# Other places for the next batch's steps in batches 1 and 2 of an attention and feed-forward kernel

## The chip, the cores and the metric

The kernel runs on one core of a Trainium2 chip. The metric is the device time of one execution in microseconds (us); lower is better.

## The reference

Attention with projected keys and values, and behind it a feed-forward layer with a hard swish. Inputs are float32; q, k and v are [8 batches, 8 heads, 1024, 64], E and F are [64, 1024], w_in is [512, 2048], w_out is [2048, 512].

```python
k_proj = einsum('ks,bhsd->bhkd', E, k)
v_proj = einsum('ks,bhsd->bhkd', F, v)
scores = matmul(q, k_proj.transpose(0, 1, 3, 2)) / sqrt(64)
attn = exp(scores - max(scores)); attn = attn / (sum(attn) + 1e-09)
x = matmul(attn, v_proj).transpose(0, 2, 1, 3).reshape(8192, 512)
h = x @ w_in
out = (h * clip(h + 3.0, 0.0, 6.0) / 6.0) @ w_out
```

## The kernel before

The kernel works through the batches b = 0 to 7, each in two halves t = 0 and 1 of 512 tokens. While TensorE computes the feed-forward layer of batch b, the attention of batch b + 1 (`second`, a few steps for b + 2 as `third`) is put between its steps. Everything is issued in the order of the program; each engine takes its instructions in that order and waits by semaphores.

**The order.** A half is a written-out list of steps: `START` for the first half of batch 1, `ORDER` for the others of batches 1 and 2, `QUADS` from batch 3 on.

```python
    ORDER = ("L0 A7 L1 A6 L2 B7 L3 A1 L4 B2 L5 A3 L6 B5 L7 A4 "
             "L8 L9 B6 L10 N2 L11 B1 L12 N5 L13 B3 L14 L15 B4").split()
    START = "L0 B3 L1 L2 B4 L3 L4 L5 L6 L7 L8 L9 L10 N2 L11 L12 L13 N5 L14 L15".split()
```

- `Ln` is block n of 16 of the first layer (`first_group`): 8 matmuls of 128x64 weights by 512 tokens into a PSUM bank `mm` (four banks, the one that was freed first is taken next); then relu on ScalarE into `r` (L562), and on VectorE the product `g` (L563), which frees the bank. In batches up to 3, L0 and L1 of the first half are split: L0 takes the first three quarters of the contraction for two blocks (12 matmuls, two banks, xT of head pairs 0 to 2), L1 the last quarter of both (4 matmuls, head pair 3).
- `An`, `Bn` and `Nn` are the seven products (Strassen's) of the second layer for a pair of output blocks, 16 matmuls with 256 columns each. A and B belong to the half before, N to this one. Products 7, 2, 5 go to an `at` bank (four banks), which ScalarE copies (`m`, L692). Products 6, 1, 3, 4 add up in one `mm` bank, which VectorE reads between them: `o_sb<-m,mm` behind 6 and 1, `o_sb<-mm,m` behind 3; so 1 waits for the reading behind 6, 3 for that behind 1, 4 for that behind 3. A7 reads the half before's last eight blocks of `g`, block 15 last.
- `sums.c` (POOL, `sc<-g`, behind L7), `sums.a` (VectorE, `g<-g`: a long part behind N5 of START or B3 of ORDER, a short one at the start of the next half), `sums.b` (VectorE, `sb`) and `sums.d` (POOL, `sd`), both behind L0, make the operands of the products. `sc` is read first by N5, `sd` by A3.

**The attention of the next batch**, in the order in which it must run:

- `load_next`: POOL copies one element of the transposed queries (`mark`) and by that waits for their landing, then requests k, v (and q) of the batch after next. For batch 3, q is requested on its own (`behind_that`), behind a mark on the reciprocal sums.
- `projected`: 32 matmuls of keys and values into one `at` bank, two copies of the keys on ScalarE (`kp`), then entries in the list `later`, of which each L step issues one: `turn` (SyncE transposes `kp` into kT and q in two halves into qT, by DMA), the two copies of the values.
- `scores(j, ...)`: for each head pair j, 8 small matmuls into two `at` banks and two exponentials on ScalarE into `aT`; those of the first j at once, those of the second through `later`.
- `add_up(j)`: VectorE sums `aT` of j (`parts`, L308), after both of its exponentials.
- `spread(a, b)`: at a, VectorE turns the sums (L317 to L321); at b, it takes reciprocals (L326), and SyncE writes them to DRAM and reads them back spread over the partitions (`rec`), 8 transfers.
- `values(j)`: 4 matmuls into two `at` banks, and two multiplications by `rec` on VectorE into `xT` (L300) of the next batch.

`at((t, place), ...)` puts such steps behind a named step of half t; several at one place run in the order of their `at`.

Of the kernel before, what the change touches and what calls it, by code (L numbers as in the profile page):

```python
# [15 lines left out]
def kernel(  # L16
# [11 lines left out]
    nc = tc.nc  # L28
    B, H, S, D = q.shape
# [44 lines left out]
    def g_tile():  # L74
        return gpool.tile([P, FO, TOK], bf16, tag="g", name="g")
# [41 lines left out]
    def load_kqv(b, order="qkv"):  # L117
        kqv.setdefault(b, {})
        for n in order:
            kqv[b][n] = raw_tile(n)  # L120
            nc.gpsimd.dma_start(out=kqv[b][n], in_=kqv_dram[n][b])
# [10 lines left out]
    def add(out, x, y, engine=nc.vector):  # L132
        engine.tensor_tensor(out=out, in0=x, in1=y, op=ALU.add)  # L133

    def sub(out, x, y, engine=nc.vector):
        engine.tensor_tensor(out=out, in0=x, in1=y, op=ALU.subtract)  # L136
# [3 lines left out]
    v11, v12, v21, v22 = [w_in_sb[:, k:k + KX, f * P:(f + NQ) * P] for k in (0, KX) for f in (FO - 2 * NQ, FO - NQ)]  # L140
# [74 lines left out]
    def behind_that(last, *what):  # L215
        mark = att.tile([1, 1], bf16, tag="mark", name="mark")
        nc.gpsimd.tensor_copy(mark, last)
        load_kqv(*what)
# [3 lines left out]
    class Attention:  # L222
# [38 lines left out]
        def scores(self, j, *allocs):  # L261
            qT = qT_dma[self.b]
            tiles = [alloc() for alloc in allocs]
            for a in range(2):
                for t in range(NB):
                    for r in range(2):
                        nc.tensor.matmul(tiles[r][t * KP:(t + 1) * KP, a * HT:(a + 1) * HT],  # L267
                                         self.kT[r * D:(r + 1) * D, 2 * j + a, :],
                                         qT[r * D:(r + 1) * D, j, a, t * HT:(t + 1) * HT],
                                         start=True, stop=True)  # L270
            return tiles
# [23 lines left out]
        def values(self, j, *allocs):  # L295
            return self.quads(lambda r, h: self.vp[r:r + KP, h, :], j, allocs)
# [7 lines left out]
        def add_up(self, *js):  # L304
            if self.parts is None:
                self.parts = att.tile([P, KO, 32], f32, tag="parts", name="parts", bufs=1)
            for j in js:
                nc.vector.tensor_reduce(out=self.parts[:, j], op=ALU.add, axis=mybir.AxisListType.X, apply_transpose=True,  # L308
                                        in_=self.aT[j].rearrange("p a r n -> p (a r n)").rearrange(
                                            "p (c i) -> p c i", i=32))  # L310
# [239 lines left out]
    def behind_steps(n):  # L550
        return lambda f: soon.append([n, f])

    def step_done():
        for entry in soon:
            entry[0] -= 1
        for entry in [entry for entry in soon if entry[0] <= 0]:
            soon.remove(entry)
            entry[1]()
# [30 lines left out]
    def x_tile():  # L589
        return xpool.tile([P, KO, NB, TOK], bf16, tag="xT", name="xT")  # L590
# [42 lines left out]
    second = Attention(1)  # L633
    second.xT = x_next

    def pop():
        if later:
            later.pop(0)()
# [205 lines left out]
    second = Attention(2)  # L844
    for b in range(1, B):
        if b + 1 < B:
            x_next = second.xT = x_tile()
        third = Attention(b + 2) if b + 2 < B else None

        plan = {}  # L850

        def at(place, *what):
            plan.setdefault(place, []).extend(what)

        def scores(*js):
            return lambda: second.some_scores(js)

        def values(*js):
            return lambda: second.some_values(*js)

        def add_up(*js):
            return lambda: second.add_up(*js)

        def spread(turned, inverted):
            at(turned, lambda: second.sums_turned())
            at(inverted, lambda: second.spread_sums())

        if b == 1:
            at((0, "L2"), sums_of_w_in)
            at((0, "L0"), second.projected)  # L870
            at((0, "L8"), second.load_next)
            at((0, "N5"), scores(0, 1))
            at((0, "L15"), add_up(0))
            at((1, "L0"), add_up(1))
            at((1, "L1"), scores(2, 3))
            at((1, "L2"), add_up(2))
            at((1, "L3"), add_up(3))
            spread((1, "B2"), (1, "L5"))
        elif b == 2:
            at((0, "L2"), second.projected)  # L880
            at((0, "A4"), second.load_next)
            at((0, "A4"), scores(0, 1))
            at((0, "B6"), scores(2))
            at((0, "L10"), add_up(0))
            at((0, "B1"), scores(3), add_up(1))
            at((0, "B3"), add_up(2))
            at((1, "A6"), add_up(3))
            spread((1, "A1"), (1, "L4"))
            at((1, "L4"), third.projected)
        elif b + 1 < B:  # L890
            if b == 3:
                at((0, "L0"), lambda: add(v12, v12, v22, nc.gpsimd), lambda: sub(v21, v21, v22, nc.gpsimd))
                at((0, "start"), second.load_next)
            at((0, "L1"), scores(0, 1))
            at((0, "B7"), add_up(0))
            at((0, "A1"), scores(2, 3), add_up(1))
            at((0, "A3"), add_up(2))
            at((0, "A4"), add_up(3))
            spread((0, "B6"), (0, "B3"))
            if third:  # L900
                at((0, "B4"), lambda: third.projected(pause=False))
                if third.b + 1 < B:
                    at((1, "L7"), third.load_next)
        if b < 3:
            at((1, "N2"), values(0))
            at((1, "L12"), values(1))
            at((1, "B3"), values(2))
            at((1, "L14"), values(3))
            if b == 1:
                at((1, "B3"), lambda: behind_that(second.recs[1][:1, 0, :1], 3, "q"))  # L910
        elif b + 1 < B:
            at((1, "L3"), values(0, 1))
            at((1, "L7"), values(2, 3))

        def done(place):
            for f in plan.pop((t, place), ()):
                f()

        for t in range(NB):
            g = g_tile()  # L920
            sums = Sums(g)
            start = (b, t) == (1, 0)
            pairs = {"A": behind[0], "B": behind[1], "N": Pair(b, t, sums, 0, (b, t) == (B - 1, NB - 1))}
            quads = b > 2
            if quads:
                pairs["Q"] = Quad(xT, t, g, (b, t) == (B - 1, NB - 1))
            if not start:
                behind[0].sums.a(KH - left, KH)
            left = 2 * NQ if quads else 2
            done("start")  # L930
            for what in START if start else QUADS if quads else ORDER:
                n = int(what[1:])
                if what[0] != "L":
                    pairs[what[0]].step(n)
                    step_done()
                    if quads and what[0] in "LQB":
                        pop()
                    done(what)
                    if what == ("N5" if quads else "N5" if start else "B3"):
                        sums.a(0, KH - left)  # L940
                    continue
                if b < 4 and t == 0 and n < 2:
                    if n == 0:
                        first_two = TwoGroups(xT, t, g)
                    for fo in range(2):
                        first_two.part(fo, range(n * (KO - 1), KO - 1 + n))
                    if n == 1:
                        first_two.out()
                else:
                    first_group(xT, t, g, n, behind_steps(2) if quads and n >= KH else now)  # L950
                step_done()
                pop()
                if n == KH - 1:
                    sums.c()
                if not start and n == 0:
                    behind[0].sums.b()
                    behind[0].sums.d()
                if quads and n == 0:
                    pairs["Q"].sums()
                done(what)  # L960
            while soon:
                step_done()
            behind = [pairs["N"], Pair(b, t, sums, 1, (b, t) == (B - 1, NB - 1))]
        assert not plan, plan
        second, xT = third, x_next
# [37 lines left out]
```

## Time and profile before

| | us |
|---|---|
| median of 3 runs (480.66 to 480.93) | 480.84 |
| the profiled execution | 480.11 |
| its span, first to last instruction | 478.3 |
| PE busy in it | 471.1 |
| VectorE busy in it | 340.0 |
| POOL busy in it | 304.4 |
| ScalarE busy in it | 275.1 |

The granted TensorE clock is 1.000 over the span. PE is TensorE's matmuls, PEld its weight loads, DVE is VectorE, ACT ScalarE, POOL GpSimd, SP SyncE. A row of the timeline has the start and the length in us, the engine, the line of the kernel, the operation with what it writes and reads, and the number of instructions merged in it; in brackets stands the idle time of the engine before it and what ended it. The lengths of matmuls are modelled and overlap, so on PE the distance of the starts is the time that a step takes. A row of the form "DMA v<-in_v_dram" in the chain of waits has the start of the request and the time to the landing.

### The profile page before, as it was taken

Reading aid. Unit: us, or ns where it says so; the run is one execution under the profiler, and the core shown is the slowest. Engines: PE = TensorE matmul, PEld = TensorE weight load, DVE = VectorE, ACT = ScalarE, POOL = GpSimd, SP = SyncE. Lnnn points to the kernel's source line nnn. Section 1 sums busy time; section 2 is a strip of 40 time slices with the busy share of each in tenths; the row PEclk is TensorE's granted clock in tenths of the full one; section 3 lists DMA queues with packets and bytes.
Section 4 is the critical chain, followed back from the end, with each engine's and each line's share of the span. In section 5 each row is a group of like instructions: output and inputs, shape, how many; then the busy total and the mean of one; then the engine's idle time right before and its main releaser. Section 6 shows DMA issues by size and latency. Waiting matters only on the chain.

```text
span 478.3 us, 14964 instructions
## 1 busy us (share of the span) xinstructions
PE 471.1 (99%) x6450; PEld 347.1 (73%) x6450; DVE 340.0 (71%) x549; ACT 275.1 (58%) x532; POOL 304.4 (64%) x206
## 2 busy tenths in 40 slices
PE   8899999999999999999999999999999999999997
PEld 4454567667666776787787877778687877878797
DVE  3583387678765958886778867887778897747574
ACT  3666478775447554756466555666457554556451
POOL 8634956144335123877897778887778588788820
PEclk9999999999999999999999999999999999999999
DMA  9999989984976989995999197962931054111012
GB/s 165 197 201 207 239 148 209 161 152 95 226 148 109 208 158 223 201 202 135 222 143 194 48 210 144 209 135 67 210 117 45 24 151 120 45 47 45 30 62 89
DMA packets 84593, 68.65 MB, mean 144 GB/s; under 512 B 38320, under 2 KB 70576, under 8 KB 84528
## 3 DMA queue, kind: packets, MB, share of 16 engines
q0 software_dynamic: 33008, 29.36, 39.4%
q1 hardware_dynamic: 51152, 37.83, 33.0%
q8 instruction: 50, 0.82, 0.7%
q10 hardware_dynamic: 368, 0.52, 0.4%
q14 instruction: 15, 0.12, 0.1%
HBM read 71.83 MB, written 16.97 MB: 186 GB/s over the span
## 4 chain that ended last, share of the span: by engine, by line
PE 82%; DMA 7%; DVE 4%; POOL 2%; ACT 2%; issue 2%; SPq 1%; POOLq 0%; ACTq 0%
PE mm L199 60%; PE at L199 19%; DMA v<-in_v_dram 5%; DMA rec<-turned_rows 1%; PE at L288 1%; DVE g L563 1%; PE at L267 1%; DVE parts L308 1%; ACT aT L276 1%; SPq L335 1%; POOL q L103 1%; POOL k L107 1%; DMA turned_rows<-inv 0%; POOL v L107 0%; DVE xT L300 0%
## 5 line engine op out<-in xcount | busy, mean ns | idle before, releaser
L199 PE MATMUL mm<-xT,w_in_sb 128*64 128x512 bf16 (+1 forms) x1808 | 222.3, 375 | 0.0
L563 DVE SCALAR_TENSOR_TENSOR g<-r,mm 128x512 bf16<-128x512 f32 x216 | 146.1, 680 | 70.8 <-ACT r L562 69.8
L562 ACT ACTIVATE r<-mm 128x512 f32<-128x512 f32 x216 | 128.3, 598 | 114.6 <-PE mm L199 109.0
L199 PEld LDWEIGHTS <-w_in_sb 128*64 128x64 bf16 x2048 | 118.9, 110 | 58.3 <-issue 3.2
L199 PEld LDWEIGHTS <-g 128*64 128x64 bf16 x2048 | 113.5, 110 | 23.9 <-issue 4.1
L133 POOL TENSOR_TENSOR sc<-g 128x2048 bf16<-128x2048 bf16 x14 | 57.0, 4072 | 53.0 <-DVE g L563 53.0
L136 POOL TENSOR_TENSOR sd<-g,sb 128x1024 bf16<-128x1024 bf16 x28 | 59.0, 2126 | 42.4 <-DVE sb L136 40.0
L199 PE MATMUL mm<-w_out_sb,g 128*64 128x256 bf16 (+1 forms) x1088 | 78.1, 286 | 0.1
L199 PE MATMUL at<-w_sums,g 128*64 128x256 bf16 x896 | 59.0, 273 | 0.2 <-DVE g L563 0.2
L776 POOL TENSOR_SCALAR r<-r 128x512 f32<-128x512 f32 x27 | 41.5, 1536 | 15.2 <-ACT r L771 15.2
L692 ACT COPY m<-at 128x256 f32<-128x256 f32 x84 | 31.3, 373 | 32.8 <-PE at L199 28.1
L777 POOL TENSOR_TENSOR g<-r,qm 128x512 bf16<-128x512 f32 x27 | 36.3, 1345 | 2.3
L300 DVE TENSOR_TENSOR xT<-at,rec 128x512 bf16<-128x512 f32 x54 | 34.9, 682 | 2.6 <-DMA rec<-turned_rows 1.9
L199 PE MATMUL mm<-w_out_sb,sd 128*64 128x256 bf16 x480 | 31.4, 273 | 0.1
L136 DVE TENSOR_TENSOR o_sb<-m,mm 128x256 f32<-128x256 f32 x60 | 24.7, 412 | 9.5 <-PE mm L199 7.2
L199 PE MATMUL mm<-w_sums,sb 128*64 128x256 bf16 x480 | 31.3, 273 | 0.0
L276 ACT ACTIVATE aT<-at 128x512 bf16<-128x512 f32 x52 | 29.5, 602 | 2.9 <-PE at L267 2.9
L199 PEld LDWEIGHTS <-sd 128*64 128x64 bf16 x480 | 26.9, 110 | 4.0 <-issue 0.4
L308 DVE TRANSPOSE_TENSOR_REDUCE parts<-aT 128x32 f32<-128x1024 bf16 x24 | 29.6, 1234 | 0.0
L199 PE MATMUL at<-w_out_sb,sc 128*64 128x256 bf16 x448 | 29.6, 273 | 0.0
L199 PEld LDWEIGHTS <-sc 128*64 128x64 bf16 x480 | 26.7, 110 | 3.6 <-issue 0.5
L199 PEld LDWEIGHTS <-sb 128*64 128x64 bf16 x480 | 26.2, 110 | 4.2 <-issue 1.9
(115 smaller groups left out, 496.1 us busy)
## 6 DMA issues: line engine op xcount, KB each, us to landing
out_dram<-o_sb SPq DMA_DIRECT2D x60, 256.0 KB, 4.4
rec<-turned_rows SPq DMA_DIRECT2D x48, 256.0 KB, 5.8
k<-in_k_dram POOLq DMA_DIRECT2D x7, 1024.0 KB, 10.6
v<-in_v_dram POOLq DMA_DIRECT2D x7, 1024.0 KB, 16.3
q<-in_q_dram POOLq DMA_DIRECT2D x7, 1024.0 KB, 21.1
w_out_sb<-in_moe_w_out_dram POOLq DMA_DIRECT2D x4, 512.0 KB, 15.0
w_in_sb<-in_moe_w_in_dram POOLq DMA_DIRECT2D x7, 256.0 KB, 9.7
k<-in_k_dram POOLq DMA_DIRECT2D x4, 256.0 KB, 5.6
```

Source lines behind the costliest of these rows:

```text
L103: nc.gpsimd.dma_start(out=q0[:, t, hs], in_=kqv_dram["q"][0][:, hs, t * SB:(t + 1) * SB, :])
L133: engine.tensor_tensor(out=out, in0=x, in1=y, op=ALU.add)
L136: engine.tensor_tensor(out=out, in0=x, in1=y, op=ALU.subtract)
L199: nc.tensor.matmul(ps[lo:lo + width], stationary[:, lo:lo + width], moving, **flags)
L276: when(lambda r=r: nc.scalar.activation(aT[:, :, r, :], tiles[r].rearrange("p (a n) -> p a n", a=2), AF.Exp, scale=scale))
L300: when(lambda t=t: nc.vector.tensor_mul(self.xT[:, j, t, :], av[t], rec[:, t]))
L308: nc.vector.tensor_reduce(out=self.parts[:, j], op=ALU.add, axis=mybir.AxisListType.X, apply_transpose=True, in_=self.aT[j].rearrange("p a ...
L562: nc.scalar.activation(r, h_ps, AF.Relu, bias=0.5, scale=1.0 / 6.0)
L563: when(lambda: nc.vector.scalar_tensor_tensor(g[:, fo, :], r, 1.0, h_ps, op0=ALU.min, op1=ALU.mult))
L692: self.copy(m, ps)
L776: nc.gpsimd.tensor_scalar(out=r, in0=r, scalar1=1.0, scalar2=None, op0=ALU.min)
L777: nc.gpsimd.tensor_tensor(out=g, in0=r3, in1=h3, op=ALU.mult)
```

## The change

For the next batch's steps in batch 1 and in batch 2, the change gives other places in the lists. `ORDER`, `START` and all the steps themselves stay.

| step | batch 1 before | batch 1 after | batch 2 before | batch 2 after |
|---|---|---|---|---|
| projection of b + 1 | t0 L0 | t0 L6 | t0 L2 | t0 L0 |
| load_next | t0 L8 | t0 L12 | t0 A4 | t0 A1 |
| scores(0,1) | t0 N5 | t0 L14 | t0 A4 | t0 L9 |
| scores 2 and 3 | t1 L1 | t1 L1 | t0 B6; t0 B1 | t0 L14, as one |
| add_up(0), (1), (2), (3) | t0 L15, t1 L0, L2, L3 | t0 L14, t1 L0, L2, L3 | t0 L10, B1, B3, t1 A6 | t0 B6, N5, B4, t1 L1 |
| spread | t1 B2, L5 | t1 A1, B2 | t1 A1, L4 | t1 A1, B2 |
| values(0), (1), (2), (3) | t1 N2, L12, B3, L14 | t1 N2, B3, B3, B4 | t1 N2, L12, B3, L14 | t1 B1, N5, L13, B4 |
| q of batch 3 | t1 B3 | t1 B4 | | |
| projection of b + 2 | | | t1 L4 | t1 L6 |
| sums of w_in | t0 L2 | t0 B4 | | |

In batch 3, two operations of POOL on `w_in` go from t0 L0 to t0 A6. The condition `quads` is written in another way and is true in the same halves. The diff, with batch 3's lines and the conditions cut:

```diff
         if b == 1:
-            at((0, "L2"), sums_of_w_in)
-            at((0, "L0"), second.projected)
-            at((0, "L8"), second.load_next)
-            at((0, "N5"), scores(0, 1))
-            at((0, "L15"), add_up(0))
+            at((0, "B4"), sums_of_w_in)
             at((1, "L0"), add_up(1))
+            at((0, "L14"), scores(0, 1))
             at((1, "L1"), scores(2, 3))
+            at((1, "N2"), values(0))
+            at((0, "L12"), second.load_next)
+            at((0, "L14"), add_up(0))
             at((1, "L2"), add_up(2))
             at((1, "L3"), add_up(3))
-            spread((1, "B2"), (1, "L5"))
+            spread((1, "A1"), (1, "B2"))
+            at((1, "B4"), values(3))
+            at((0, "L6"), second.projected)
+            at((1, "B3"), values(1))
+            at((1, "B3"), values(2))
+            at((1, "B4"), lambda: behind_that(second.recs[1][:1, 0, :1], 3, "q"))
         elif b == 2:
-            at((0, "L2"), second.projected)
-            at((0, "A4"), second.load_next)
-            at((0, "A4"), scores(0, 1))
-            at((0, "B6"), scores(2))
-            at((0, "L10"), add_up(0))
-            at((0, "B1"), scores(3), add_up(1))
-            at((0, "B3"), add_up(2))
-            at((1, "A6"), add_up(3))
-            spread((1, "A1"), (1, "L4"))
-            at((1, "L4"), third.projected)
+            at((0, "B4"), add_up(2))
+            at((0, "B6"), add_up(0))
+            at((0, "L0"), second.projected)
+            at((0, "L9"), scores(0, 1))
+            at((1, "B4"), values(3))
+            at((1, "B1"), values(0))
+            at((0, "A1"), second.load_next)
+            spread((1, "A1"), (1, "B2"))
+            at((0, "L14"), scores(2, 3))
+            at((1, "L6"), third.projected)
+            at((0, "N5"), add_up(1))
+            at((1, "L1"), add_up(3))
+            at((1, "L13"), values(2))
+            at((1, "N5"), values(1))
...
-        if b < 3:
-            at((1, "N2"), values(0))
-            at((1, "L12"), values(1))
-            at((1, "B3"), values(2))
-            at((1, "L14"), values(3))
-            if b == 1:
-                at((1, "B3"), lambda: behind_that(second.recs[1][:1, 0, :1], 3, "q"))
```

More of the change, by code (lines that the diff above doesn't have):

```diff
@@ L868 @@
         if b == 1:
-            at((0, "L2"), sums_of_w_in)
-            at((0, "L0"), second.projected)
-            at((0, "L8"), second.load_next)
-            at((0, "N5"), scores(0, 1))
-            at((0, "L15"), add_up(0))
+            at((0, "B4"), sums_of_w_in)
             at((1, "L0"), add_up(1))
+            at((0, "L14"), scores(0, 1))
             at((1, "L1"), scores(2, 3))
+            at((1, "N2"), values(0))
+            at((0, "L12"), second.load_next)
+            at((0, "L14"), add_up(0))
             at((1, "L2"), add_up(2))
             at((1, "L3"), add_up(3))
-            spread((1, "B2"), (1, "L5"))
-        elif b == 2:
-            at((0, "L2"), second.projected)
-            at((0, "A4"), second.load_next)
-            at((0, "A4"), scores(0, 1))
-            at((0, "B6"), scores(2))
-            at((0, "L10"), add_up(0))
-            at((0, "B1"), scores(3), add_up(1))
-            at((0, "B3"), add_up(2))
-            at((1, "A6"), add_up(3))
-            spread((1, "A1"), (1, "L4"))
-            at((1, "L4"), third.projected)
+            spread((1, "A1"), (1, "B2"))
[4 more added lines that the diff above has]
+            at((1, "B4"), lambda: behind_that(second.recs[1][:1, 0, :1], 3, "q"))
+        elif b == 2:
+            at((0, "B4"), add_up(2))
[12 more added lines that the diff above has]
+            at((1, "N5"), values(1))
         elif b + 1 < B:
             if b == 3:
-                at((0, "L0"), lambda: add(v12, v12, v22, nc.gpsimd), lambda: sub(v21, v21, v22, nc.gpsimd))
                 at((0, "start"), second.load_next)
@@ L903 @@
                     at((1, "L7"), third.load_next)
-        if b < 3:
-            at((1, "N2"), values(0))
-            at((1, "L12"), values(1))
-            at((1, "B3"), values(2))
-            at((1, "L14"), values(3))
-            if b == 1:
-                at((1, "B3"), lambda: behind_that(second.recs[1][:1, 0, :1], 3, "q"))
-        elif b + 1 < B:
+        if 2 < b < B - 1:
             at((1, "L3"), values(0, 1))
             at((1, "L7"), values(2, 3))
+        if b == 3:
+            at((0, "A6"), lambda: add(v12, v12, v22, nc.gpsimd), lambda: sub(v21, v21, v22, nc.gpsimd))
         def done(place):
@@ L923 @@
             pairs = {"A": behind[0], "B": behind[1], "N": Pair(b, t, sums, 0, (b, t) == (B - 1, NB - 1))}
-            quads = b > 2
+            quads = (b, t) >= (3, 0)
             if quads:
```

## The prediction

> **What bounds the kernel now.** I read the page first.
>
> ```profile
> span 478.3 us, 14964 instructions
> PE 471.1 (99%) x6450; PEld 347.1 (73%) x6450; DVE 340.0 (71%) x549; ACT 275.1 (58%) x532; POOL 304.4 (64%) x206
> ```
>
> PE is busy 99% of the span, and the change removes no matmul and adds none. So it can win only what PE loses between its steps in batches 1 and 2, and lose only by new waits there. The next view is therefore the timeline of PE over those batches, read by the starts of rows (ends overlap). Columns: start, length, engine, line, operation, operands, count.
>
> ```profile
> 98.48 1.04 PE L199 MATMUL at<-w_out_sb,sc 128*64 128x256 bf16 x16
> 99.45 0.94 PE L267 MATMUL at<-qT,kT 64*64 64x256 bf16 x16
> 100.32 2.78 PE L199 MATMUL mm<-xT,w_in_sb 128*64 128x512 bf16 x24
> 102.93 1.13 PE L199 MATMUL at<-w_sums,g 128*64 128x256 bf16 x16
> 103.90 1.03 PE L199 MATMUL mm<-xT,w_in_sb 128*64 128x512 bf16 x8
> 104.86 0.63 PE L267 MATMUL at<-qT,kT 64*64 64x256 bf16 x16
> 105.42 1.06 PE L199 MATMUL mm<-w_out_sb,g 128*64 128x256 bf16 x16
> ...
> 111.62 1.06 PE L199 MATMUL mm<-xT,w_in_sb 128*64 128x512 bf16 x8
> 112.79 1.06 PE L199 MATMUL mm<-w_out_sb,sd 128*64 128x256 bf16 x16
> ...
> 115.40 1.06 PE L199 MATMUL mm<-xT,w_in_sb 128*64 128x512 bf16 x8
> 116.58 1.06 PE L199 MATMUL mm<-w_out_sb,g 128*64 128x256 bf16 x16
> ```
>
> These are, in order, N5, scores(0,1), L14 with L15 and the next L0 (24 matmuls), A7, L1, scores(2,3), A6, then L5, A3, L7, A4 of batch 1. Three L steps take 102.93 - 100.32 = 2.61 us, so a step is 0.87 us; a product step streams as many columns and takes the same. Whatever exceeds 0.87 is loss. After L5, A3 should start at 112.49 and starts at 112.79: 0.30 lost. A4 should start at 116.27 and starts at 116.58: 0.31 lost. A7 takes 0.97: 0.10 lost. A visit of two score groups costs 105.42 - 103.90 - 0.87 = 0.65 undisturbed, but 100.32 - 98.48 - 0.87 = 0.97 behind N5: 0.32 lost. A loss of this kind is all the change can move.
>
> **Visits put together.** The same timeline, later: B3 to L14 with one values visit between; B6 to L10 with one score group; an L step and the product after it, with two values groups between (batch 3).
>
> ```profile
> 127.07 1.04 PE L199 MATMUL mm<-w_out_sb,sd 128*64 128x256 bf16 x16
> ...
> 128.38 1.05 PE L199 MATMUL mm<-xT,w_in_sb 128*64 128x512 bf16 x8
> ...
> 149.88 1.04 PE L199 MATMUL mm<-w_out_sb,g 128*64 128x256 bf16 x16
> ...
> 151.19 1.05 PE L199 MATMUL mm<-xT,w_in_sb 128*64 128x512 bf16 x8
> ...
> 225.46 1.03 PE L199 MATMUL mm<-xT,w_in_sb 128*64 128x512 bf16 x8
> ...
> 226.97 1.06 PE L199 MATMUL mm<-w_sums,sb 128*64 128x256 bf16 x16
> ```
>
> A single visit costs 1.31 - 0.87 = 0.44 of either kind, two together 1.51 - 0.87 = 0.64: every visit pays about 0.2 for turning to the smaller tiles and back. Batch 2's scores(2,3) as one visit save 2 x 0.44 - 0.65 = 0.23. Batch 1's values(1) and values(2), now both at B3, save 0.24. **-0.47.**
>
> **Batch 1, first half.** scores(0,1) goes from behind N5 to behind L14. Its 0.32 was a wait for N5's bank, which ScalarE copies while L14 now runs: gone. What is late next is L15's product on VectorE, because add_up(0) is now queued ahead of it (it was queued behind it) and waits for both exponentials.
>
> ```profile
> 99.90 1.08 ACT L276 ACTIVATE aT<-at 128x512 bf16<-128x512 f32 x2
> 101.42 0.60 ACT L562 ACTIVATE r<-mm 128x512 f32<-128x512 f32 x1 [0.43 <-PE mm L199]
> ...
> 103.02 0.69 DVE L563 SCALAR_TENSOR_TENSOR g<-r,mm 128x512 bf16<-128x512 f32 x1 [0.29 <-ACT r L562]
> 103.63 1.24 DVE L308 TRANSPOSE_TENSOR_REDUCE parts<-aT 128x32 f32<-128x1024 bf16 x1
> ```
>
> The first two rows are of the timeline of ScalarE, the others of VectorE. Relu follows an L step by 0.23 (L14 ended at 101.19). New order: N5 ends 99.35, L14 100.22, visit 100.87, L15 101.74, L0 102.61; A7 reads L15's block in its last eighth, 103.37. Relu of L14 100.45; exponentials start about 0.49 later and 0.49 apart, the second ends 102.0; add_up(0) 102.05 to 103.25; L15's product ends 103.9. A7 loses 0.6 where 0.32 + 0.10 was lost: **+0.2**. The wait has no cover on PE. Its ends are 0 (the sum fits into VectorE's idle time) and 1.24 (all of it stands ahead); the worked value lies between.
>
> scores(0,1) also needs kT and the first half of qT, and the projection moves from L0 to L6.
>
> ```profile
> 85.30 1.06 ACT L241 CAST kp<-at 64x512 bf16<-64x512 f32 x2 [3.06 <-PE at L199]
> 139.21 1.23 SPq L250 DMA_TRANSPOSE kT<-kp  x1
> DMA to landing us min/median/max: 4.5/6.0/9.2
> ```
>
> The rows: ScalarE's copies of the keys, SyncE's issue of kT, and the answer for the tile qT. From the projection's end to scores(0,1) are ten steps, 8.7 us; the chain is 0.24 + 1.06 + 1.23 + 6.0 and some 0.1 of handover, 8.6. I take no further wait from the median (k and v of batch 3 are requested only when it has landed); at 9.2 it would be 3 us, at 4.5 none. The Trainium skill's page "DMA: Bandwidth & Descriptors", section "Latency and other measured facts", gives DMA transposes 261 GB/s; by it a half (512 KB) would land in an estimated 2.0 us and this wait be impossible. The trace's shortest is 4.5, so the trace decides and the wait stays a rival.
>
> **Batch 1, second half.** A3 and A4 wait for VectorE to read the bank that they add to: both start as the subtraction before them ends.
>
> ```profile
> 112.36 0.38 DVE L136 TENSOR_TENSOR o_sb<-m,mm 128x256 f32<-128x256 f32 x1
> ...
> 116.17 0.35 DVE L136 TENSOR_TENSOR o_sb<-mm,m 128x256 f32<-128x256 f32 x1
> ```
>
> VectorE is behind there because four sums of 1.24 lie in its queue. The change starts the first at 102.05 instead of 103.63. Chaining the same operations at the pitch of before, L15's product ends at 103.9 as it did (103.71), but one sum is then already done: everything behind is about 1.0 us earlier, while PE is 0.2 later. Then A1's subtraction ends at 112.1 (needed 112.6), A3's at 115.95 (needed 116.1). The turned sums move to A1 and the reciprocal to B2, ahead of L4's and L5's products; their banks are wanted a microsecond later still. Both waits go, the second narrowly: **-0.6** (ends 0 and -0.7). The spread's transfers start about 1.2 earlier; values(0), which is not moved, only gains.
>
> **From batch 1 to 2.** PE from L0 of batch 2, then VectorE before it.
>
> ```profile
> 131.47 1.47 PE L199 MATMUL mm<-xT,w_in_sb 128*64 128x512 bf16 x12
> 132.76 0.94 PE L199 MATMUL at<-w_sums,g 128*64 128x256 bf16 x14
> 133.88 0.30 PE L199 MATMUL at<-w_sums,g 128*64 128x256 bf16 x2 [0.19 <-DVE g L563]
> 134.02 0.60 PE L199 MATMUL mm<-xT,w_in_sb 128*64 128x512 bf16 x4
> ...
> 128.35 0.68 DVE L563 SCALAR_TENSOR_TENSOR g<-r,mm 128x512 bf16<-128x512 f32 x1
> ...
> 129.29 1.29 DVE L300 TENSOR_TENSOR xT<-at,rec 128x512 bf16<-128x512 f32 x2
> 130.49 0.95 DVE L136 TENSOR_TENSOR g<-g 128x1536 bf16<-128x1536 bf16 x1
> 131.36 0.68 DVE L563 SCALAR_TENSOR_TENSOR g<-r,mm 128x512 bf16<-128x512 f32 x1
> ```
>
> A7 takes 1.26: 0.39 lost, since values(3)'s multiplications stood ahead of L15's product. They now stand behind it, and the projection of batch 3 (L0 instead of L2) lies between L0 and A7: gone. But values(1) and values(2) put four multiplications and the long subtraction between L13's and L14's products, and the second of L0's two banks is L14's. From L13's end: its product starts at 0.88 (relu 0.23 + 0.60), B3's subtraction at 1.48, the multiplications from 1.82, 0.60 apart, to 4.22, the subtraction to 5.09, L14's product ends at 5.77. PE: B3, visit 0.64, L14, L15, B4, visit 0.44, half of L0's 1.29: 5.2. A wait of 0.6 for 0.39 removed: **+0.2** (ends -0.4 and +0.9).
>
> **Batch 2.** The chain of waits has the load of batch 4's v; POOL's timeline the sum queued at the same place; PE the projection that reads v.
>
> ```profile
> 153.36 16.16 DMA v<-in_v_dram
> 148.32 4.07 POOL L133 TENSOR_TENSOR sc<-g 128x2048 bf16<-128x2048 bf16 x1 [8.38 <-DVE g L563]
> 169.12 0.38 PE L199 MATMUL at<-k,e_t 128*64 128x512 bf16 x1
> 169.56 0.38 PE L199 MATMUL at<-v,f_t 128*64 128x512 bf16 x1
> ```
>
> PE waits 0.44 for v, less some 0.05 that the two halves overlap. load_next moves from A4 to A1, ahead of sc on POOL, and the projection from L4 to L6. load_next waits there for the second half of qT, landing near 145 (projection ends 134.3, copies, kT, two transposes); v, 16.2 after its request near 146, lands at 162, the projection starts near 171. sc, held behind load_next's wait and three requests (about 0.9 each), ends near 152; N5 wants it near 154. So the wait goes, **-0.4**, with 2 us of cover on POOL. In the second half add_up(3) stands before A6's subtraction; the same chain as in batch 1, add_up(2) and (3) included, frees A1's bank within 0.1 of its need: **+0.05** (to +0.3). values(3) at B4 is read only in L1, two steps on. The sums of w_in, the request for batch 3's q (B3 to B4) and batch 3's two POOL operations (L0 to A6) pass nothing in POOL's queue and cost nothing; were POOL late there, their readers are eight steps away.
>
> **Sum.** -0.47 + 0.2 - 0.6 + 0.2 - 0.4 + 0.05 = -1.0 us. The profiled execution took 480.11, so 479.1 on its scale; the median of the runs is 0.73 above it, 480.84, so **479.8**. From batch 3 on PE is as full as before, and the shift passes to the end.
>
> **Rivals.** A measurement of this kernel can tell about 0.2%, 0.96 us, from no change; the forecast lies just on it.
> 1. VectorE's backlog stays: add_up(0) blocks longer than worked out, and A3's and A4's waits stay (0.6). For it: margins of 0.15 to 0.5. Against: one sum really runs in idle time. 480.4. Chance 0.17.
> 2. The two new waits are shorter than worked out (the four multiplications start sooner, L15's product is through in time): 0.8 less. For it: they hang on chains of five or six pitches. 479.0. Chance 0.18.
> 3. Slower: the first half of qT lands late in batch 1, and PE stands at L14 with everything behind it. From 8 us of landing on the sum is above +0.9; at 9.2 it is +2, 482.8. For it: the maximum 9.2, and no slack in the ten steps. Against: the median 6.0, q itself long loaded, no other load in flight. POOL's sc in batch 2 has 2 us of slack against the same cause. Chance 0.1.
>
> **How the numbers follow.** Forecast 0.55, about half of it beyond 0.96 us: faster 0.29, same 0.26. Rival 2 is faster, rival 1 same. Together faster 0.47, same 0.43, slower 0.1. The range goes from just under rival 2 to above rival 1, 478.8 to 481.1, and leaves out rival 3 and the far side of rival 2.
>
> **What would show it.** Right: no gap at A3 and A4 of batch 1, v of batch 4 landed before its projection, one score visit of 16 matmuls behind L14 in batch 2; a gap of 0.6 at A7 behind L0 in batch 1 and another of 0.6 within L0 of batch 2. Wrong: a gap ahead of scores(0,1) of batch 1 with a transpose as releaser, sc of batch 2 later than N5, or either 0.6 absent.

## The result: 478.16 us, 2.3 us faster, and the profile after

The changed kernel takes 478.16 us (median; 477.90 to 478.47), against 480.48 us for the kernel before in the same comparison: ratio 0.9954, 95% interval 0.9941 to 0.9966. The forecast was 479.8, with a range from 478.8: the sign was right, the gain (2.3) was more than twice the one worked out (1.0). The profiled execution took 478.34 us, with a span of 476.5 where it was 478.3, at the same granted clock of 1.0. First the page's head:

```profile
span 476.5 us, 14965 instructions
PE 468.7 (98%) x6450; PEld 345.4 (72%) x6450; DVE 340.5 (71%) x549; ACT 274.8 (58%) x532; POOL 304.7 (64%) x206
```

The matmuls are the same 6450. Now the timeline of TensorE (start, length, engine, line, operation, operands, count) in batch 1, from N5 to A4, as the prediction showed it of before:

```profile
99.48 1.03 PE L199 MATMUL mm<-xT,w_in_sb 128*64 128x512 bf16 x8
100.44 0.63 PE L267 MATMUL at<-qT,kT 64*64 64x256 bf16 x16
101.00 1.92 PE L199 MATMUL mm<-xT,w_in_sb 128*64 128x512 bf16 x16
102.75 0.93 PE L199 MATMUL at<-w_sums,g 128*64 128x256 bf16 x14
104.03 0.30 PE L199 MATMUL at<-w_sums,g 128*64 128x256 bf16 x2 [0.35 <-DVE g L563]
104.17 1.03 PE L199 MATMUL mm<-xT,w_in_sb 128*64 128x512 bf16 x8
...
111.79 1.03 PE L199 MATMUL mm<-xT,w_in_sb 128*64 128x512 bf16 x8
112.66 1.04 PE L199 MATMUL mm<-w_out_sb,sd 128*64 128x256 bf16 x16
...
115.27 1.03 PE L199 MATMUL mm<-xT,w_in_sb 128*64 128x512 bf16 x8
116.13 1.04 PE L199 MATMUL mm<-w_out_sb,g 128*64 128x256 bf16 x16
```

These are L14, scores(0,1), L15 with L0, A7, L1, then L5, A3, and L7, A4. The score visit costs 101.00 - 99.48 - 0.87 = 0.65 (0.97 before). A7, from 102.75 to 104.17, takes 1.42 instead of 0.87, with L15's product on VectorE as its releaser: some 0.5 lost (the last two matmuls start 0.52 later than the pace of the fourteen before them would have it). A3 starts 0.87 after L5 and A4 0.86 after L7: both waits are gone.

The same timeline from B3 of batch 1 to A7 of batch 2, and the rows of VectorE and ScalarE that belong to it:

```profile
126.14 1.04 PE L199 MATMUL mm<-w_out_sb,sd 128*64 128x256 bf16 x16
127.11 0.63 PE L288 MATMUL at<-aT,vp 64*64 64x512 bf16 x8
127.66 1.92 PE L199 MATMUL mm<-xT,w_in_sb 128*64 128x512 bf16 x16
129.41 1.04 PE L199 MATMUL mm<-w_out_sb,g 128*64 128x256 bf16 x16
130.38 0.41 PE L288 MATMUL at<-aT,vp 64*64 64x512 bf16 x4
130.72 1.49 PE L199 MATMUL mm<-xT,w_in_sb 128*64 128x512 bf16 x12
132.04 0.38 PE L199 MATMUL at<-k,e_t 128*64 128x512 bf16 x1
...
133.77 1.04 PE L199 MATMUL at<-w_sums,g 128*64 128x256 bf16 x16
...
127.98 2.47 DVE L300 TENSOR_TENSOR xT<-at,rec 128x512 bf16<-128x512 f32 x4
130.37 0.95 DVE L136 TENSOR_TENSOR g<-g 128x1536 bf16<-128x1536 bf16 x1
131.23 1.27 DVE L563 SCALAR_TENSOR_TENSOR g<-r,mm 128x512 bf16<-128x512 f32 x2
...
130.50 0.37 ACT L730 COPY o_sb<-mm 128x256 f32<-128x256 f32 x1 [0.21 <-DMA out_dram<-o_sb]
```

values(1) and values(2) are one visit of 0.65. L0 of batch 2 (12 matmuls from 130.72) runs without a gap into the projection, though VectorE comes as worked out: four multiplications, the long subtraction, and L14's and L15's products from 131.23. The forecast wait of 0.6 within L0 is not there. A7 starts at 133.77 without its old 0.39.

Last, batch 2: the second score visit, the projection that reads v of batch 4, and sc on GpSimd.

```profile
156.60 1.03 PE L199 MATMUL mm<-xT,w_in_sb 128*64 128x512 bf16 x8
157.56 0.63 PE L267 MATMUL at<-qT,kT 64*64 64x256 bf16 x16
158.12 1.05 PE L199 MATMUL mm<-xT,w_in_sb 128*64 128x512 bf16 x8
...
170.30 1.03 PE L199 MATMUL mm<-xT,w_in_sb 128*64 128x512 bf16 x8
171.16 0.38 PE L199 MATMUL at<-k,e_t 128*64 128x512 bf16 x1
171.16 0.38 PE L199 MATMUL at<-v,f_t 128*64 128x512 bf16 x1
...
148.89 4.10 POOL L133 TENSOR_TENSOR sc<-g 128x2048 bf16<-128x2048 bf16 x1
```

scores(2,3) are one visit of 0.65, the projection starts on both k and v as L6 ends, and sc ends at 152.99, a microsecond ahead of N5 (153.99).

**A scale for the rest.** The executions differ already in the way to the loop: the point in batch 0 at which 386 us of matmuls are left (counted by the columns that they stream) was reached between 78.14 and 78.96 us in the fourteen profiled executions, whatever the kernel. The time from that point to the end of the span is a finer measure of one trace, and the experiments are read by it ("behind the start" in the table): 399.73 before and 397.85 after, **1.88 less**. The medians differ by 2.3, and the interval of the ratio, times 480.5, is 1.6 to 2.8: the trace's 1.88 lies inside. From the start of batch 3 to the end the two traces run in step to 0.02, so all of the 1.88 is won in batches 1 and 2.

### The profile page after: what moved, and what is told of

It reads as the page before. It is cut to its first block, busy times and chain, and to the rows that moved or that the text cites. A ratio compares the mean times of both kernels' runs of the same rounds, so it can differ in the third digit from the quotient of the medians.

```text
span 476.5 us, 14965 instructions
## 1 busy us (share of the span) xinstructions
PE 468.7 (98%) x6450; PEld 345.4 (72%) x6450; DVE 340.5 (71%) x549; ACT 274.8 (58%) x532; POOL 304.7 (64%) x206
## 4 chain that ended last, share of the span: by engine, by line
PE 93%; DMA 2%; ACT 2%; POOL 2%; DVE 0%; issue 0%; POOLq 0%
PE mm L199 69%; PE at L199 21%; DMA v<-in_v_dram 2%; PE at L288 2%; PE at L267 1%; ACT aT L276 1%; POOL q L103 1%; POOL k L107 1%; POOL v L107 0%; PE at L457 0%; DVE parts L308 0%; ACT rec L211 0%; ACT rec L205 0%; ACT m L692 0%; PE at L437 0%
## 5 line engine op out<-in xcount | busy, mean ns | idle before, releaser
L563 DVE SCALAR_TENSOR_TENSOR g<-r,mm 128x512 bf16<-128x512 f32 x216 | 146.0, 681 | 71.4 <-ACT r L562 70.4
L199 PEld LDWEIGHTS <-w_in_sb 128*64 128x64 bf16 x2048 | 117.3, 110 | 58.8 <-issue 3.0
L308 DVE TRANSPOSE_TENSOR_REDUCE parts<-aT 128x32 f32<-128x1024 bf16 x24 | 29.6, 1235 | 0.3 <-ACT aT L276 0.3
```

The costliest lines, as they stand in the source:

```text
L199: nc.tensor.matmul(ps[lo:lo + width], stationary[:, lo:lo + width], moving, **flags)
L563: when(lambda: nc.vector.scalar_tensor_tensor(g[:, fo, :], r, 1.0, h_ps, op0=ALU.min, op1=ALU.mult))
```

## Experiments

**Theory 1:** the gain is the sum of waits and visits, each with its own place, and L0's wait failed to come because its second bank was another one than assumed. **Rivals:** one edit carries it all, or the wait for v is larger in other executions than in the profiled one; L0's wait failed because VectorE was faster; or the larger gain of the medians comes from batch 3, where the change also moved GpSimd's work. (Of the last, the two traces show one thing already: on GpSimd the two moved operations run behind xd and ahead of sc before and after, so the move passes nothing in its queue.) The first four kernels do one part alone on the kernel before, and pool_adds_early alters it too; the others alter the changed kernel. They were timed in four comparisons, in which the kernel before had other medians (480.21 for the first four; 480.46 for after_again, second_bank, sum_behind_product and pool_adds_early; 480.68 for the last; 480.26 for the rest), so medians of different comparisons are compared by their ratios.

| kernel | median us | ratio to before, 95% | behind the start, to before |
|---|---|---|---|
| v_wait_alone | 479.77 | 0.9989 (0.998 to 0.9998) | -0.37 |
| first_sum_alone | 479.39 | 0.9984 (0.9975 to 0.9994) | -0.95 |
| last_values_alone | 479.92 | 0.9994 (0.9985 to 1.0003) | -0.40 |
| one_score_visit_alone | 480.29 | 0.9999 (0.999 to 1.0008) | +1.58 |
| after_again | 478.14 | 0.9954 (0.9941 to 0.9966) | -1.90 |
| second_bank | 478.82 | 0.9966 (0.9953 to 0.9978) | -1.28 |
| sum_behind_product | 478.45 | 0.9957 (0.9944 to 0.9971) | -1.69 |
| pool_adds_early | 480.29 | 0.9998 (0.9989 to 1.0007) | -0.01 |
| later_sums | 478.32 | 0.9961 (0.9948 to 0.9973) | -2.10 |
| values_at_b3 | 478.40 | 0.9964 (0.995 to 0.9977) | -1.97 |
| all_three | 479.14 | 0.9979 (0.997 to 0.9988) | -0.76 |
| later_sums_load_behind_sc | 478.43 | 0.9963 (0.9948 to 0.9978) | -2.04 |

The intervals of last_values_alone, one_score_visit_alone and pool_adds_early hold 1, and those of the kernels that alter the changed kernel by a few tenths overlap its own: what is said of such parts rests on one trace each.

**v_wait_alone**, on the kernel before:

```diff
-            at((1, "L4"), third.projected)
+            at((1, "L6"), third.projected)
```

> The kernel before with one move: the projection of batch 4 from L4 to L6 of batch 2's second half. Theory 1 (the gain is the sum of PE's waits that the trace of before shows): the 0.44 us between the projection's first key matmul and its first value matmul goes, time -0.4 us, nothing else changes. Theory 2 (the times gain 2.3 us where the two traces differ by 1.8, because the wait for v is often longer than in the one profiled execution): -0.8 us or more, and the runs lie closer together than those of the kernel before.

The timeline of TensorE in that kernel, L6 and the first two matmuls of the projection:

```profile
171.44 1.03 PE L199 MATMUL mm<-xT,w_in_sb 128*64 128x512 bf16 x8
172.30 0.38 PE L199 MATMUL at<-k,e_t 128*64 128x512 bf16 x1
172.31 0.38 PE L199 MATMUL at<-v,f_t 128*64 128x512 bf16 x1
```

The wait is gone without load_next being moved at all, and the other waits stay: 0.37 of the trace's gain. The executions spread as widely as before (479.12 to 480.75), so the wait for v is not what makes the spread (it does vary: 0.44 in the trace of before, 0.70 in that of one_score_visit_alone).

**first_sum_alone**, on the kernel before:

```diff
-            at((0, "N5"), scores(0, 1))
-            at((0, "L15"), add_up(0))
+            at((0, "L14"), scores(0, 1), add_up(0))
```

> The kernel before with scores(0,1) and add_up(0) of batch 1 both behind L14 (were N5 and L15). Theory 1 (VectorE's backlog): the waits of 0.30 and 0.31 us at A3 and A4 and 0.1 at A1 of batch 1 go, A7 behind L0 waits 0.5 instead of 0.1, the wait of 0.3 within scores(0,1) goes: -0.6 us. Rival (the waits go because the turned sums and the reciprocal moved, not because the first sum starts earlier): A3 and A4 keep their waits of 0.3, and the time is +0.1 us.

The timeline of TensorE, A7 of batch 1:

```profile
102.30 0.93 PE L199 MATMUL at<-w_sums,g 128*64 128x256 bf16 x14
103.58 0.30 PE L199 MATMUL at<-w_sums,g 128*64 128x256 bf16 x2 [0.35 <-DVE g L563]
```

A7 loses the same 0.52 as in the changed kernel, and the waits of A1, A3 and A4 are gone with the turned sums still in their old place. A7's 0.39 in batch 2 went too: with the sums ready earlier, VectorE no longer waits for the reciprocals ahead of values(1) (0.31 at 127.15 before), and all that follows on it is earlier. This one edit is half of the trace's whole gain (0.95 of 1.88).

**last_values_alone**, on the kernel before, for batch 1 only:

```diff
-            at((1, "L14"), values(3))
+            at((1, "B4" if b == 1 else "L14"), values(3))
```

> The kernel before with values(3) of batch 1 behind B4 (was L14). Theory 1 (A7 waits because values(3)'s two multiplications stand ahead of L15's product on VectorE): A7's wait of 0.39 us at the start of batch 2 goes, time -0.4 us, with no projection between L0 and A7. Rival (the projection put between L0 and A7 is what hides it): most of the 0.39 stays here, time -0.1 to 0.

A7 of batch 2 follows L0 without a gap, although no projection stands between them here; the waits of A3, A4 and v stay. So values(3) behind L15's product is enough, as the prediction had it (-0.40 in the trace). first_sum_alone removes the same wait, so the two may not be added.

**one_score_visit_alone**, on the kernel before, in batch 2:

```diff
-            at((0, "B6"), scores(2))
-            at((0, "B1"), scores(3), add_up(1))
-            at((0, "B3"), add_up(2))
-            at((1, "A6"), add_up(3))
+            at((0, "L14"), scores(2, 3))
+            at((0, "B1"), add_up(1))
+            at((0, "B4"), add_up(2))
+            at((1, "L1"), add_up(3))
```

> The kernel before with batch 2's scores(2) and scores(3) as one visit behind L14, add_up(2) behind B4 and add_up(3) behind L1. Theory 1: one turn to the small tiles and back less, -0.2 us, and no new wait of more than 0.1 at A1 of the second half. Rival (two sums close together put VectorE behind at A1 and A3 of the second half, as in batch 1): waits of 0.2 to 0.4 there, time 0 to +0.3 us.

The visit is there (0.65), and A1 and A3 of the second half wait for nothing, so the expected rival did not come. But the median does not show the visit's 0.2, and the profiled execution (481.28, the slowest of eleven) lost some 1.8 us elsewhere: 0.38 in batch 1, ahead of the edit, where values(1) waited behind late reciprocals, 0.26 more at v, and most of it, 1.3, in batch 3. The timelines of GpSimd, VectorE and TensorE in batch 3 of that execution:

```profile
208.61 4.05 POOL L133 TENSOR_TENSOR sc<-g 128x2048 bf16<-128x2048 bf16 x1
...
209.96 2.79 DVE L320 COPY turned<-turned 32x128 f32<-32x128 f32 x1
...
214.38 0.63 PE L199 MATMUL mm<-xb,v_sums 128*64 128x256 bf16 x8 [0.80 <-DVE qm L136]
215.31 1.06 PE L199 MATMUL mm<-w_out_sb,sd 128*64 128x256 bf16 x16 [0.30 <-DVE o_sb L136]
```

and in the changed kernel, VectorE's copy:

```profile
208.38 1.44 DVE L320 COPY turned<-turned 32x128 f32<-32x128 f32 x1
```

The second half of qT landed late, everything on GpSimd came later, sc ran until 212.66, and VectorE's small copy ended only then, TensorE behind it. This suggested the third rival for the difference between medians and trace; pool_adds_early shortens this chain in the kernel before.

**pool_adds_early**, on the kernel before:

```diff
-                at((0, "L0"), lambda: add(v12, v12, v22, nc.gpsimd), lambda: sub(v21, v21, v22, nc.gpsimd))
+                at((0, "start"), lambda: add(v12, v12, v22, nc.gpsimd), lambda: sub(v21, v21, v22, nc.gpsimd))
                 at((0, "start"), second.load_next)
```

> The kernel before, with GpSimd's two operations on w_in in batch 3 (together 2.3 us) queued at the start of the batch ahead of the requests that wait for the transposed queries, instead of behind them at L0. In the profiled execution in which the queries landed latest, the sum sc ended 1.2 us later and VectorE's copy of the turned sums, and with it TensorE, was held until then (0.96 and 0.49 us lost). Theory 1 (this chain on GpSimd costs the kernel before time in a part of its executions): with 2.3 us taken out of the chain the median falls by 0.2 to 0.5 and the slowest executions, above 480.9, disappear. Rival (rare, or not the reason): median within 0.15 of the kernel before, the same spread.

The eleven executions lie closer together (480.02 to 480.70) and none is above 480.9, but the median is 0.17 below and the interval holds 1. Of the kernel before, only two of fifteen executions were above 480.9 in the same comparison, so this can be chance. That the chain on GpSimd can cost an execution time is shown by the one trace above; that it makes the median's gain larger than the trace's is not shown.

**after_again**, the changed kernel unaltered:

> The changed kernel once more, with more executions, so that its spread can be set beside that of the kernel before (479.39 to 481.38 in 33 executions). Theory 1 (the gain is the sum of waits and visits that the two traces show, about 1.8 us, and 0.3 to 0.5 more because executions in which GpSimd is late in batch 3 no longer cost TensorE time): 478.1 to 478.3, ratio 0.995, and no execution above 478.9. Theory 2 (the first comparison was lucky, the gain is the trace's 1.8 alone): 478.5 to 478.7, ratio 0.996 to 0.9965, with a spread as wide as before.

478.14, ratio 0.9954 again, and 1.90 behind the start where the first trace had 1.88: the gain stands in two separate comparisons. One of its executions was at 478.95, just over the bound named, so the spread decides nothing.

**second_bank**, on the changed kernel, for the last accumulation of batch 1 (the copy and its store are put off until L0's matmuls are issued; shortened):

```diff
-                self.copy(self.lo[:, left], self.x)
...
+                def finish():
+                    (nc.vector.tensor_copy if self.hold else self.copy)(self.lo[:, left], self.x)
...
+                if self.hold:
+                    held.append(finish)
...
+                    while held:
+                        held.pop()()
```

> The changed kernel, but the last accumulation of batch 1 (B4's bank) is copied by VectorE behind the long subtraction, instead of by ScalarE, so that the second bank of batch 2's L0 is that which L14 leaves, as the prediction assumed. Theory 1 (the forecast wait of 0.6 in L0 failed to come only because the second bank was another one): L14's product on VectorE ends near 131.9, the second group of L0 would start near 131.4, so 0.5 is lost within L0 with VectorE's product as its releaser, and the time is 0.3 to 0.5 above the changed kernel's. Rival (VectorE's chain was simply faster than worked out, the bank is beside the point): no wait in L0, the time as the changed kernel's within 0.1. The copy on VectorE (some 0.4 us) stands ahead of the subtraction for A5, five steps ahead of its reader, and should cost nothing by either.

TensorE and VectorE around L0 of batch 2:

```profile
130.97 0.84 PE L199 MATMUL mm<-xT,w_in_sb 128*64 128x512 bf16 x6
132.21 0.84 PE L199 MATMUL mm<-xT,w_in_sb 128*64 128x512 bf16 x6 [0.40 <-DVE g L563]
...
131.48 1.28 DVE L563 SCALAR_TENSOR_TENSOR g<-r,mm 128x512 bf16<-128x512 f32 x2
```

The missing wait appears: 0.57 within L0, released by VectorE's product, and the time is 0.68 above the changed kernel's (0.62 behind the start), more than the 0.3 to 0.5 expected. VectorE's rows stand at the same distance from L0's start as in the changed kernel. The bank was the reason; that VectorE was faster is refuted.

**sum_behind_product**, on the changed kernel, batch 1:

```diff
-            at((0, "L14"), add_up(0))
+            at((0, "L15"), add_up(0))
```

> The changed kernel, with add_up(0) of batch 1 at L15 instead of L14, so that it is queued behind L15's product on VectorE. Theory 1 (VectorE is full from there to A4, so what is put later comes back there): A7's wait of 0.52 goes, VectorE's queue is 0.5 later and TensorE 0.5 earlier; A3's bank, free 0.54 ahead of need, is then about 0.45 late, and A4's, free 0.22 ahead, about 0.3 late. Net 0 to +0.3. Rival (VectorE has idle time enough): A7's 0.52 goes and nothing comes back, -0.5.

TensorE at L5, A3 and L7, A4:

```profile
111.03 1.06 PE L199 MATMUL mm<-xT,w_in_sb 128*64 128x512 bf16 x8
112.20 1.06 PE L199 MATMUL mm<-w_out_sb,sd 128*64 128x256 bf16 x16
...
114.81 1.06 PE L199 MATMUL mm<-xT,w_in_sb 128*64 128x512 bf16 x8
115.98 1.06 PE L199 MATMUL mm<-w_out_sb,g 128*64 128x256 bf16 x16
```

A7's 0.52 goes and 0.31 is lost at A3 and again at A4, the waits of the kernel before. The first sum is paid on one side or the other; by the trace the place that the change chose is the cheaper by 0.2, which the medians (0.31 apart, intervals overlapping) do not settle.

**later_sums**, on the changed kernel, moves the later sums as well:

```diff
-            at((0, "L14"), add_up(0))
-            at((1, "L2"), add_up(2))
-            at((1, "L3"), add_up(3))
-            spread((1, "A1"), (1, "B2"))
-            at((1, "N2"), values(0))
+            at((0, "L15"), add_up(0))
+            at((1, "A1"), add_up(2))
+            at((1, "L4"), add_up(3))
+            spread((1, "A3"), (1, "L6"))
+            at((1, "N5"), values(0))
```

> The changed kernel, with every later step of batch 1's sums moved as well: add_up(0) behind L15's product, add_up(2) from L2 to A1, add_up(3) from L3 to L4, the turned sums from A1 to A3, the reciprocal from B2 to L6, values(0) from N2 to N5. Theory 1 (VectorE has room behind A1's subtraction, not ahead of it): A7's 0.52 goes and A3 and A4 wait for nothing, since only one sum is left ahead of A1's subtraction; 0.5 below the changed kernel, 477.7. Rival (the reciprocals come late and the values wait for them, or their results hold the banks that the projections and L steps want): a wait of 0.3 to 1 near N5 or B3 in the place of A7's, time as the changed kernel's or above.

GpSimd's sc, and TensorE's last L step ahead of N5 and N5, in batch 2:

```profile
149.79 4.10 POOL L133 TENSOR_TENSOR sc<-g 128x2048 bf16<-128x2048 bf16 x1
...
152.89 1.03 PE L199 MATMUL mm<-xT,w_in_sb 128*64 128x512 bf16 x8
153.95 1.06 PE L199 MATMUL at<-w_out_sb,sc 128*64 128x256 bf16 x16
```

All waits of batch 1 went, 0.44 less to the end of that batch; then 0.2 was lost at N5 of batch 2 for sc (it ends at 153.89), since the second half of qT landed 0.9 later and sc stands behind the requests that wait for it. The rival's time came, but not by its mechanism: it had named the reciprocals. The median is not below the changed kernel's.

**later_sums_load_behind_sc** puts load_next back at A4 in that kernel:

```diff
-            at((0, "A1"), second.load_next)
+            at((0, "A4"), second.load_next)
```

> The kernel later_sums, with batch 2's load_next back at A4, so that on GpSimd it stands behind the sum sc again and not ahead of it. In later_sums the second half of qT landed at 146.6, the three requests followed, sc ended at 153.9, and TensorE lost 0.2 at N5. Theory 1 (that is all that ate the gain of later_sums): sc starts near 148 and ends near 152.3, no loss at N5; v, requested near 153 and 16 later landed near 169, is read at L6, near 170.9, without a wait; 0.2 below later_sums, so 0.4 below the changed kernel, 477.8. Rival (v lands after 171 and the wait of the kernel before is back): 0.1 to 0.4 lost at the projection, time as later_sums or above.

Neither sc nor v is waited for now, but in this execution batch 3 lost 0.37 at the step shown (0.11 in the changed kernel), in the way shown above; VectorE's copy and TensorE:

```profile
207.86 1.70 DVE L320 COPY turned<-turned 32x128 f32<-32x128 f32 x1
...
212.13 1.06 PE L199 MATMUL mm<-w_out_sb,sd 128*64 128x256 bf16 x16 [0.20 <-DVE o_sb L136]
```

The median, 478.43, is no gain either.

**values_at_b3**, on the changed kernel, batch 2:

```diff
-            at((1, "L13"), values(2))
-            at((1, "N5"), values(1))
+            at((1, "B3"), values(1))
+            at((1, "B3"), values(2))
```

> The changed kernel, with batch 2's values(1) and values(2), which stand alone at N5 and L13, both at B3 as in batch 1. Theory 1 (a visit costs 0.2 whatever stands beside it): 0.2 less, and the 0.1 lost ahead of B4 goes as the multiplications of values(2) no longer stand ahead of L14's subtraction on VectorE; 477.9 to 478.0. Rival (the multiplications now pile up behind B3 and L0 of batch 3, whose bank is not that of the accumulation, waits for them): a new wait of 0.3 to 0.6, time 0.1 to 0.4 above the changed kernel.

Both happened: the visit and B4's wait were saved (0.38 up to batch 3), then 0.25 was lost ahead of L1 of batch 3, for the bank that values(3)'s multiplications free. Nothing is left of it in the median.

**all_three**: the edits of later_sums and values_at_b3 together, and batch 3's two GpSimd operations from A6 to the start, ahead of load_next.

> The two edits of the kernels later_sums and values_at_b3 together, and GpSimd's two operations on w_in in batch 3 at the start of the batch, ahead of the requests. Theory 1 (each wait has its own place, gains add): 0.7 to 0.8 below the changed kernel, 477.4. Rival (a gain in batch 1 brings TensorE sooner to what batch 2 and 3 wait for): less than 0.5 in all, with a wait for qT or v back in batch 2 or 3.

A loss, for a third reason. VectorE and GpSimd at the end of batch 2:

```profile
189.24 1.95 DVE L136 TENSOR_TENSOR g<-g 128x1536 bf16<-128x1536 bf16 x1
...
189.22 1.15 POOL L136 TENSOR_TENSOR w_in_sb<-w_in_sb 128x512 bf16<-128x512 bf16 x1
```

The subtraction that takes 0.95 elsewhere took 1.95, beside one of GpSimd's that began 0.02 earlier and ran until 190.37. That GpSimd's held it is read from these times (the last section has more of the kind). Everything on VectorE was a microsecond later, and A7 and L1 of batch 3 lost 1.25. In batch 1 the reciprocals came late too (0.41 in L0 of batch 2).

## Why the prediction was right or wrong

**What bounds the kernel, and the visits:** right. Each of the two joined visits costs 0.65, the one of batch 1's values and the one of batch 2's scores.

**Batch 1, first half:** right in place and releaser; A7 loses 0.52 where 0.6 was worked out, so about +0.1 instead of +0.2. Rival 3 did not come: the transposes of qT landed in 4.4 to 5.1 us there (4.7 in the median), less than the 6.0 reckoned with, and in the same 4.4 to 5.1 in every other trace in which batch 1's projection stands at L6. The 2.0 us that the prediction estimated from the rate on the Trainium skill's page "DMA: Bandwidth & Descriptors", section "Latency and other measured facts", was not reached in any of them.

**Batch 1, second half:** right, and somewhat larger: A3's and A4's 0.31 each are gone, and 0.10 at A1 that the prediction had left out. The two subtractions that free the banks end at 112.17 and 115.95 (112.1 and 115.95 forecast). first_sum_alone shows that the earlier first sum does it.

**From batch 1 to 2: the step that failed** is "the second of L0's two banks is L14's". The forecast chain on VectorE came true to a tenth (L14's product ends near 131.85, 1.1 after L0 starts). But the second bank was the one of the accumulation that B4 ends: it was the next to come free, copied by ScalarE from 130.50 to 130.87, 0.5 ahead of need. The trace agrees: the first matmul on L0's second bank waits for a semaphore that ScalarE raises in the changed kernel, and for one that VectorE raises in the kernel before and in second_bank. I had carried the assignment of the kernel before over to a kernel in which the order of releases is another. Instead of +0.2 this part gave -0.39, and second_bank, which brings L14's bank back, brings 0.57 of wait back. That is 0.6 of the 0.9 by which the trace's gain exceeds the forecast.

**Batch 2:** right. The wait for v is gone with sc 1.0 ahead of its reader (2 forecast, since the second half of qT landed at 145.7 and sc ended at 152.99). v_wait_alone shows that the projection's two steps alone would have done. Not foreseen was a loss of 0.11 ahead of B4 in the second half, behind the multiplications of values(2); the 0.05 at A1 did not come.

**The sum:** -0.47 + 0.1 - 0.72 - 0.39 - 0.39 + 0.11 = -1.76, against 1.88 in the trace; 0.1 is not assigned. The parts tried alone give the same: 0.95 (first_sum_alone, with A7's wait of batch 2 in it), 0.37 for v and the two visits' 0.47 are 1.79. **The scale** was off as well: I put the median 0.73 above the profiled execution, from three runs at 480.66 to 480.93. In the five comparisons made since, the kernel before had medians of 480.21 to 480.68, and the changed kernel's profiled execution lies 0.2 above its median. Of the 1.6 between 479.8 and 478.16, 0.9 is the trace's and 0.7 to 0.8 is this. Whether a part of it is a gain in batch 3 that the two traces don't show stays open; pool_adds_early, which puts the two operations earlier than either kernel has them, moved the median by 0.17, within noise.

**Rivals:** rival 2 came nearest, since one of the two new waits is absent; its reason (shorter chains) was wrong, and the chances (0.47 for faster) were too low by what one wrong bank costs, and because the 0.96 us by which they were split was too wide: the measured interval is 0.6 us to either side. Rival 1 is refuted by A3 and A4.

## What to carry to other kernels

Where a forecast wait hangs on which buffer comes next from a rotating pool, work out the order of releases in the new program, and give both buffers as cases. A wait that is removed is worth its length only up to the next late thing: here five further edits each removed the wait they aimed at, and 0.2 to 1.3 us came back at sc, at the next bank, or in batch 3. Before a fine sum is put on the median's scale, ask how far single executions differ ahead of the part in question.

## What the runs showed of the hardware

Some of VectorE's work between tiles in SBUF was held while GpSimd computed, and some was not. GpSimd and VectorE in batch 3 of the changed kernel, ahead of the copy of 1.44 us shown above:

```profile
205.67 4.07 POOL L133 TENSOR_TENSOR sc<-g 128x2048 bf16<-128x2048 bf16 x1 [1.28 <-DVE g L563]
...
205.51 1.24 DVE L308 TRANSPOSE_TENSOR_REDUCE parts<-aT 128x32 f32<-128x1024 bf16 x1
208.03 0.30 DVE L317 STREAM_TRANSPOSE turned<-parts 128x128 f32<-128x128 f32 x1
```

The copy L320 (32x128) takes 0.22 us in batches 1 and 2, and 1.44, 1.70 and 2.79 us where sc was running on GpSimd, each time until sc had ended (209.82 for 209.74, 209.56 for 209.49, 212.75 for 212.66); the 128x1536 subtraction took 1.95 instead of 0.95 beside a GpSimd operation that began 0.02 earlier; and the 128x2048 operation sb of the changed kernel 1.22 in the nine cases alone and 1.82 to 2.25 in the six beside GpSimd. The Trainium skill's page "SBUF — State Buffer", section "Who interferes with whom", calls the port pair that the two engines share an exclusive lock; the rows of L320 agree, the copy waits for the whole other operation and does not merely slow down. Not held beside sc were the transposing sum L308 (1.24, as elsewhere), the transposition L317 (0.30, as elsewhere), and the products that read PSUM (L563, 0.66 to 0.69).
